# Filler matmuls against a falling TensorE clock, and a late load of the last output weights, in a decode attention kernel

## The chip, the cores and the metric

The kernel runs on one core of a Trainium2 chip. The time is the device time of one execution in microseconds (us). A profiled execution gives a trace whose span is 1.7 to 2.1 us shorter than that time; all readings at a point of time below count from the start of that span. Ratios are computed as the mean time of one kernel's fast runs over the mean of the other's fast runs in the same rounds on the same chip, so they are not quite the ratio of the medians that are quoted.

Engine names: PE is TensorE (PEld its weight loads), DVE is VectorE, ACT is ScalarE, POOL is GpSimd, SP is SyncE, which issues most of the loads.

## The reference, cut to what matters

Two attention blocks for decoding one token, batch 4, 32 query heads, 8 key/value heads of 128. Block A attends to all 8192 cached keys, block B to the last 2048. Each ends with an output projection `wo` to 512 columns.

```python
q = (x @ wq) ...                                    # 32 heads of 128
scores = einsum("bhqd,bhkd->bhqk", q, k) * Dh**-0.5 # k: (4, 8, 8192, 128), repeated 4 times over the heads
p = softmax(scores);  o = einsum("bhqk,bhkd->bhqd", p, v)
return o.reshape(B, 1, 32 * 128) @ wo               # wo: (4096, 512)
# ... block B the same with k[:, :, -2048:], v[:, :, -2048:];  the two outputs side by side
```

The caches are read once; with the weights the DMA engines move 185 MB. There is almost no arithmetic for each byte.

## The kernel before

The work is cut into 40 *units*. Units 0 to 7 are block B, units 8 to 39 are block A, one for each pair of batch row and key/value head: 2 MB of K and 2 MB of V. Unit 39 is called `L`. In each unit PE transposes K in eight jobs `T` of 1024 keys, as float32 pairs, into one of three PSUM banks; DVE and ACT by turns copy the result to SBUF; then come the scores `S` (with the query columns as the moving operand, 8 columns wide). Softmax follows on DVE, POOL and ACT, and the V products `PV` (4 columns wide) of a unit run inside the next unit.

```python
TOKENS = [("T", 0), ("T", 1), ("OT",), ("T", 2), ("T", 3), ("S", 0), ("S", 1), ("X",),
          ("T", 4), ("T", 5), ("S", 2), ("S", 3), ("PV", 0), ("PV", 1), ("OL",),
          ("T", 6), ("T", 7), ("S", 4), ("S", 5), ("PV", 2), ("PV", 3), ("S", 6), ("S", 7), ("OPJ",)]

def pe_T(u, k):
    # ... bank, slot
    def fn(pe):
        ins = None
        for pi in range(4):
            t0 = k * 8 + 2 * pi
            ins = pe.transpose(out=bkf[:, pi * 128:(pi + 1) * 128],
                               in_=K_sbf[:, slot, t0:t0 + 2, :].rearrange("p t d -> p (t d)"), identity=identf[:, :])
        return ins
    op("pe", fn, waits=[("K", u) if k == 0 else None, bankfree(idx), ("setup",)], inc=("T", idx))
```

Every fourth unit (13, 17, ..., 37) also transposes the attention output of a finished group of four units (`OT`, `OL`) and multiplies it by that group's output weights (`OPJ`, four matmuls of 512 columns). It is called a *group unit* here. Unit 37, the third last, is one. Units 10 to 37 are one loop on PE, four units a turn.

After the last unit PE finishes without further transposes. Each of the last unit's four V chunks has a semaphore of its own:

```python
for c in range(NQ): pe_PV(L - 1, c)
add(dve_norm(L - 1))
for c in range(NQ): pe_PV(L, c)
add(dve_norm(L))
pe_OPJ(L // Bn)                       # the direct form: two halves of 256 columns, four heads each
# ... add of each half to the other groups' sum, and two output DMAs

for hf in range(2):                   # the direct form in pe_OPJ
    # four matmuls, one for each head, into the bank of half hf
    op("pe", fn2, waits=[...norms of the four units..., ("W1", 3), ...], inc=("OPJ", gi, hf))
```

The last group's output weights (512 KB) are loaded from ACT's queue in unit 8, far ahead. K and V pass through SP's queue in order: ..., K of 37, V of 36, K of 38, K of 39, V of 37, V of 38, V of 39 in four chunks. A K slot (one of the four buffers for a unit's K) is free when the transposes of four units earlier are done.

```python
wo_at = {7: [1, 2], 8: [NG - 1]}      # NG - 1 is the last group
```

Of the kernel before, what the change touches and what calls it, by code (L numbers as in the profile page):

```python
# [14 lines left out]
def bass_concat_heads__gqa_block_cached__sliding_block_cached__decode_kernel(  # L15
# [15 lines left out]
    Bn, _, D = A_x.shape  # L31
    _, HKV, SK, DH = A_k_cache.shape
# [61 lines left out]
    with ExitStack() as es:  # L94
# [8 lines left out]
        def sm(name):  # L103
            return es.enter_context(nc.semaphore(name))
# [40 lines left out]
        sem_k = [sm("s_k%d" % i) for i in range(NKS)]  # L145
        sem_v = [sm("s_v%d" % i) for i in range(NVS)]
        sem_vl = [sm("s_vl%d" % i) for i in range(NQ)]
        sem_x = [sm("s_x0"), sm("s_x1")]
        sem_w1 = [sm("s_w1_%d" % i) for i in range(NQP)]
        s_w2 = sm("s_w2")  # L150
# [16 lines left out]
        def bank_f(i):  # L167
            return banks_f[i]
# [16 lines left out]
        def sem_of(key):  # L185
            t = key[0]
            if t in ("K", "Kh"):
                return sem_k[key[1] % NKS]
            if t in ("V", "Vh"):
                return sem_v[key[1] % NVS]  # L190
            if t == "VL":
                return sem_vl[key[1]]
            if t == "x":
                return sem_x[key[1]]
            if t == "out":
                return sem_out[key[1]]
            if t == "W1":
                return sem_w1[key[1]]
            if t == "wo":
                return sem_w1[2]  # L200
            if t == "pm":
                return s_pm if key[2] == 0 else s_pm2
            if t == "E":
                if jobs[key[1]]["kind"] in ("xT", "QP", "perm"):
                    return s_Eq
                return s_Ed if evac_eng[key[1]] == "dve" else s_Ea
            return {
                "W2": s_w2, "T": s_T, "S": s_S, "PV": s_PV, "OPJ": s_OPJ,
                "max": s_max, "sub": s_sub, "sum": s_sum, "rcp": s_rcp, "otr": s_otr,
                "ocp": s_ocp, "exp": s_exp, "ar1": s_ar1, "ar2": s_ar2, "setup": s_setup, "pset": s_setup,  # L210
                "mk": s_mk, "acp": s_acp, "mk0": s_mk0, "perm": s_perm, "rq": s_rq, "OPJc": s_opc,
            }[t]

        DMA_KEYS = ("K", "Kh", "V", "Vh", "VL", "x", "out", "W1", "W2", "wo", "mk")

        plan = {e: [] for e in ("sp", "pe", "act", "dve", "pool")}

# [2 lines left out]
        def op(eng, fn, waits=(), inc=None):  # L220
            plan[eng].append(dict(fn=fn, waits=[w for w in waits if w is not None], inc=inc, turn=turn[0]))

        def add(d):
            op(d["eng"], d["fn"], waits=d["waits"], inc=d["inc"])
# [63 lines left out]
        def pe_job_perm(P):  # L288
# [26 lines left out]
                return ins  # L315
            return dict(eng="dve", fn=efn, waits=[("T", idx)], inc=("E", idx))

        def pe_T(u, k):
            eng = "dve" if k % 2 == 0 else "act"
            idx = new_job("T", eng, u=u, k=k)  # L320
            tjob_idx[(u, k)] = idx
            tj = u * NB + k
            bk = bank_bf(KTB[jobs[idx]["bank"]])
            slot = u % NKS

            bkf = bank_f(KTB[jobs[idx]["bank"]])

            def fn(pe):
                ins = None
                for pi in range(4):  # L330
                    t0 = k * 8 + 2 * pi
                    ins = pe.transpose(out=bkf[:, pi * 128:(pi + 1) * 128],  # L332
                                       in_=K_sbf[:, slot, t0:t0 + 2, :].rearrange("p t d -> p (t d)"),
                                       identity=identf[:, :])
                return ins
            op("pe", fn, waits=[("K", u) if k == 0 else None, bankfree(idx), ("setup",)], inc=("T", idx))

            def efn(e):
                if eng == "dve":
                    return e.tensor_copy(out=KT_sb.bitcast(I32)[:, tj % NKT, :], in_=bkf.bitcast(I32)[:, :])  # L340
                return e.activation(out=KT_sb[:, tj % NKT, :], in_=bk[:, :], func=ACTF.Copy)  # L341
            return dict(eng=eng, fn=efn, waits=[("T", idx)], inc=("E", idx))
# [114 lines left out]
        def pe_OPJ(gi):  # L457
            u0 = gi * Bn
            un = units[u0]
            P, nhq, hq0 = un["P"], un["nhq"], un["hq0"]  # L460
            opb = bank_f(OPB)
            wo_view, wg = wo_of(gi)
            first = (gi == first_group[P])
            last = (gi == last_group[P]) or gi == NG - 2
            direct = u0 + Bn - 1 == L

            if direct:
                H2 = D // 2
                for hf in range(2):
                    def fn2(pe, hf=hf):  # L470
                        ins = None
                        dst = opb[0:Bn, 0:H2] if hf == 0 else bank_f(STB[0])[0:Bn, 0:H2]
                        for i in range(nhq):
                            ins = pe.matmul(out=dst, lhsT=OTg[:, i, :], rhs=wo_view[:, wg, i, hf * H2:(hf + 1) * H2],  # L474
                                            start=(i == 0), stop=(i == nhq - 1))
                        return ins
                    op("pe", fn2, waits=[norm_key[u0 + b] for b in range(Bn)] + [("W1", 3), ("acp",), ("sub", L - 1), ("sub", L)], inc=("OPJ", gi, hf))
                return

            def fn(pe):  # L480
                ins = None
                for i in range(nhq):
                    ins = pe.matmul(out=opb[0:Bn, 0:D], lhsT=OL[:, i // REP, i % REP, :], rhs=wo_view[:, wg + i // REP, i % REP, :],  # L483
                                    start=(P == 1 and first and i == 0), stop=(P == 1 and last and i == nhq - 1))
                return ins
            waits = [("E", ol_idx[gi]), ("W2", gi) if P == 1 else ("wo", gi)]
            op("pe", fn, waits=waits, inc=("OPJ", gi))
# [97 lines left out]
        def dve_norm(u):  # L585
            un = units[u]
            b, nhq, NC = un["b"], un["nhq"], un["S"] * un["CPT"]
            gi = u // Bn
            otb = bank_f(OTB[un["ot_use"] % 2])

            def fn(dve):
                return dve.tensor_tensor(out=OTg[:, 0:nhq, b], in0=otb[:, 0:NC], in1=rl_view(u),  # L592
                                         op=AluOpType.mult)
            norm_key[u] = ("otr", u)
            ot_uses[un["ot_use"]] = ("otr", u)
            return dict(eng="dve", fn=fn, waits=[("PV", u * NQ + NQ - 1), ("rcp", u)], inc=("otr", u))
# [65 lines left out]
        def wo_load(eng, gi):  # L662
            un = units[gi * Bn]
            P, ng, r0 = un["P"], un["nhq"] // REP, un["hq0"] * DH
            view, wg = wo_of(gi)
            src = WO[P][r0:r0 + ng * REP * DH, :]
            src = src.rearrange("(h p) n -> p h n", p=128) if gi == NG - 1 else src.rearrange("(g p r) n -> p g r n", p=128, r=REP)
            dst = view[:, wg, :, :] if gi == NG - 1 else view[:, wg:wg + ng, :, :]
            waits = []
            if gi > 0:  # L670
                waits.append(("T", qp_idx[(0, NQP - 1)]))
            if NG_B < gi < NG - 1:
                waits.append(("OPJ", gi - 1))
            key = ("W2", gi) if P == 1 else (("W1", 3) if gi == NG - 1 else ("wo", gi))
            return dict(eng=eng, fn=dma(dst, src), waits=waits, inc=key)

        wo_at = {7: [1, 2], 8: [NG - 1]}
        for gi in range(NG_B + 1, NG - 1):
            wo_at[4 * gi + 2] = [gi]

# [123 lines left out]
        add(dve_norm(L - 1))  # L804
        for c in range(NQ):
            pe_PV(L, c)
        add(dve_norm(L))
        pe_OPJ(L // Bn)
        H2 = D // 2
# [28 lines left out]
        for u in range(1, NU + 1):  # L838
            if u < L:
                sp_K(u)  # L840
                if u == L - 1:
                    sp_K(L)
            if u != L:
                sp_V(u - 1)
            else:
                sp_V(L - 1)
            if u == 1:
                add(wo_load("sp", 0))
            if u == 2:
                op("sp", dma(W1wq, WQ[0].rearrange("(p c) n -> p c n", p=128)),  # L850
                   waits=[("T", qp_idx[(1, NQP - 1)])], inc=("W1", 1))
            if u == outb_after:
                op("sp", dma(out[:, 0, D:2 * D], osb[0:Bn, 1, :]), waits=[("ocp", 1)], inc=("out", 1))
        op("sp", dma(out[:, 0, 0:H2], osb[0:Bn, 0, 0:H2]), waits=[("ocp", 0)], inc=("out", 0))
        op("sp", dma(out[:, 0, H2:D], osb[0:Bn, 0, H2:D]), waits=[("ocp", 2)], inc=("out", 2))

# [134 lines left out]
```

## Time and profile before

| | before |
|---|---|
| time, median | 449.64 us (448.83 to 449.87, 3 runs) |
| span of the profiled run | 447.8 us |
| DMA busy | 90% or more in slices 2 to 39 of 40 |
| PE busy, mean clock 150 to 410 us | 237 of 260 us, 0.79 |

The page's slices (40 equal parts of the span, 11.2 us each; digits are tenths, PEclk is the clock that TensorE was granted, GB/s what the DMA engines moved):

```profile
PE   0685199899676999988998998899889998988997
PEclk9996569989886899866596689867875986788596
DMA  8999999999999999999999999999999999999991
GB/s 337 411 415 438 413 421 415 420 421 423 423 422 421 425 422 425 424 429 427 427 427 430 430 424 426 430 428 427 429 426 427 426 430 429 426 424 430 430 403 65
```

The load stream is full from the second slice to the 39th. PE follows it with a clock that falls again and again. The windows view of the same kernel gives, for each stretch, its length, busy time and number of instructions of PE, PEld, DVE, ACT, POOL, the granted clock, the DMA share and GB/s:

```profile
core 0: us, PE busy (x) PEld busy (x) DVE busy (x) ACT busy (x) POOL busy (x), PEclk, DMA share, GB/s
150.00:410.00 260.00, 237.20 (x4351) 220.96 (x4350) 116.75 (x270) 117.02 (x133) 24.96 (x80) 0.79 1.01 427
410.00:424.00 14.00, 12.37 (x184) 10.47 (x180) 6.05 (x16) 4.40 (x5) 1.31 (x4) 0.60 1.00 426
```

The chain of waits (the work that ended last, followed back; start, length, what) has its last DMA here; after it there is nothing but PE and what PE waits for on other engines:

```profile
380.50 30.60 DMA K_sb<-in_A_k_cache_dram
...
411.14 1.11 PE ps L332 x8
```

PE's timeline from there (start, length, line, operation, operands, number; in brackets the idle time before it and what ended it). L332 are the transposes, L397 the V products, L474 the output matmuls:

```profile
411.14 1.09 PE L332 MATMUL ps<-identf,K_sb 128*128 128x128 f32 x8 [0.79 <-DMA K_sb<-in_A_k_cache_dram]
413.35 1.97 PE L332 MATMUL ps<-identf,K_sb 128*128 128x128 f32 x8 [0.41 <-ACT KT_sb L341]
...
424.83 2.69 PE L332 MATMUL ps<-identf,K_sb 128*128 128x128 f32 x16
...
431.81 2.08 PE L332 MATMUL ps<-identf,K_sb 128*128 128x128 f32 x16
...
438.96 0.39 PE L397 MATMUL ps<-PT,V_sb 128*128 128x4 bf16 x10
440.17 3.31 PE L397 MATMUL ps<-PT,V_sb 128*128 128x4 bf16 x118 [0.82 <-issue]
443.79 1.86 PE L474 MATMUL ps<-W,OTg 128*4 128x256 bf16 x8 [0.31 <-DVE OTg L592]
```

Read it so: the K tile of group unit 37 is there at 411.14. The unit lasts until 424.83, 13.7 us, because its transposes run at the half clock (1.97 us for eight, against 1.07 to 1.09 at the full one). Units 38 and 39 start at 424.83 and 431.81 and take 7 us each. The two last runs of V products begin at 438.96, the output matmuls at 443.79.

How late is that against the data? The fine DMA slices from 436 to 448 us (0.3 us each) show the engines running dry one after the other, the last at about 440:

```profile
DMA  7776675443333100010000000000000000000000
```

So at 443.8 PE is several microseconds behind the data. The tail, from 411 to the end, is bound by PE, in unit 37 and in the last products at a low clock.

### The profile page before, as it was taken

How to read it: one execution, taken by the hardware profiler on the slowest of the kernel's cores; microseconds unless marked ns; L12 is line 12 of the kernel's file. 1: busy time of each engine (PE TensorE's matmuls, PEld its weight loads, DVE VectorE, ACT ScalarE, POOL GpSimd, SP SyncE). 2: the span in 40 equal slices, each digit the busy share in tenths (PEclk: the TensorE clock that was granted, in tenths of full speed). 3: DMA queues.
4: the chain of work that ended last, by engine and by line, in shares of the span. 5: the costliest groups of instructions: out<-in, count | busy, mean ns of one | idle time of the engine just before them, and what ended most of it. 6: DMA issues, size and time to landing. Idle time of an engine off the chain costs nothing.

```text
span 447.8 us, 14767 instructions
## 1 busy us (share of the span) xinstructions
PE 373.4 (83%) x6783; PEld 339.4 (76%) x6783; DVE 195.9 (44%) x451; ACT 179.2 (40%) x202; POOL 40.1 (9%) x126
## 2 busy tenths in 40 slices
PE   0685199899676999988998998899889998988997
PEld 0685199768561898878898887879878987878896
DVE  0354055656440455434363444344443544344363
ACT  1163045435330464434264434334442543435261
POOL 1100000001100011000010001000110100010010
PEclk9996569989886899866596689867875986788596
DMA  8999999999999999999999999999999999999991
GB/s 337 411 415 438 413 421 415 420 421 423 423 422 421 425 422 425 424 429 427 427 427 430 430 424 426 430 428 427 429 426 427 426 430 429 426 424 430 430 403 65
DMA packets 17270, 185.01 MB, mean 413 GB/s; under 512 B 1860, under 2 KB 2392, under 8 KB 4824
## 3 DMA queue, kind: packets, MB, share of 16 engines
q1 hardware_dynamic: 15096, 178.27, 94.4%
q10 hardware_dynamic: 2080, 6.30, 3.5%
q8 instruction: 22, 0.36, 0.3%
q14 instruction: 8, 0.07, 0.0%
q0 software_dynamic: 64, 0.01, 0.0%
HBM read 184.56 MB, written 0.01 MB: 412 GB/s over the span
## 4 chain that ended last, share of the span: by engine, by line
DMA 54%; PE 35%; issue 4%; ACT 3%; DVE 2%; POOL 0%; ACTq 0%; POOLq 0%
DMA K_sb<-in_A_k_cache_dram 41%; PE ps L332 19%; DMA W<-in_A_wq_dram 7%; DMA W<-in_B_wo_dram 6%; PE ps L397 6%; PE ps L371 5%; PE ps L483 3%; ACT KT_sb L341 3%; PE ps L278 1%; DVE KT_sb L340 1%; DVE Dt L543 0%; DVE M L505 0%; ACT PT L554 0%; PE ps L474 0%; PE ps L438 0%
## 5 line engine op out<-in xcount | busy, mean ns | idle before, releaser
L341 ACT ACTIVATE KT_sb<-ps 128x1024 bf16<-128x1024 bf16 x160 | 163.0, 1023 | 244.9 <-PE ps L332 243.1
L332 PE MATMUL ps<-identf,K_sb 128*128 128x128 f32 x1280 | 217.1, 329 | 32.9 <-DMA K_sb<-in_A_k_cache_dram 17.5
L332 PEld LDWEIGHTS ps<-identf,K_sb 128*128 128x128 f32 x1280 | 179.0, 170 | 46.2 <-DMA K_sb<-in_A_k_cache_dram 18.6
L340 DVE COPY KT_sb<-ps 128x512 int32<-128x512 int32 x160 | 110.4, 690 | 138.9 <-PE ps L332 137.7
L397 PE MATMUL ps<-PT,V_sb 128*128 128x4 bf16 (+1 forms) x2560 | 76.2, 165 | 3.6 <-DMA V_sb<-in_A_v_cache_dram 1.8
L371 PEld LDWEIGHTS ps<-RQc,KT_sb 128*128 128x128 bf16 x2048 | 72.9, 100 | 4.5 <-ACT KT_sb L341 1.2
L371 PE MATMUL ps<-RQc,KT_sb 128*128 128x8 bf16 x2048 | 74.3, 167 | 0.9 <-ACT KT_sb L341 0.8
L397 PEld LDWEIGHTS ps<-PT,V_sb 128*128 128x128 bf16 x2560 | 70.8, 97 | 3.9 <-DMA V_sb<-in_A_v_cache_dram 2.0
L575 POOL PARTITION_ALL_REDUCE LB<-L x40 | 17.3, 432 | 155.2 <-DVE L L566 155.2
L514 POOL PARTITION_ALL_REDUCE MB<-M x32 | 11.9, 371 | 173.3 <-DVE M L505 173.3
L483 PE MATMUL ps<-W,OL 128*4 128x512 bf16 x60 | 22.5, 537 | 4.8 <-DMA W<-in_B_wo_dram 4.8
L592 DVE TENSOR_TENSOR OTg<-ps,RL 128x4 bf16<-128x4 f32 (+1 forms) x40 | 6.9, 173 | 40.2 <-PE ps L397 40.2
L505 DVE TENSOR_REDUCE M<-ps 128x4 f32<-128x256 f32 (+1 forms) x40 | 19.1, 477 | 10.8 <-PE ps L371 10.8
L566 DVE TENSOR_REDUCE L<-PT 128x4 f32<-128x256 bf16 (+1 forms) x40 | 21.9, 547 | 3.3 <-ACT PT L554 2.8
L371 PE MATMUL ps<-RQB,KT_sb 128*128 128x16 bf16 x512 | 18.6, 171 | 2.1 <-issue 1.2
L371 PEld LDWEIGHTS ps<-RQB,KT_sb 128*128 128x128 bf16 x512 | 17.9, 99 | 3.0 <-issue 1.5
L554 ACT ACTIVATE PT<-Dt 128x256 bf16<-128x256 f32 (+1 forms) x40 | 18.1, 452 | 4.0 <-DVE Dt L543 2.0
L483 PEld LDWEIGHTS ps<-W,OL 128*4 128x4 bf16 x60 | 5.6, 104 | 15.3 <-issue 8.7
L278 PE MATMUL ps<-xT,W 128*128 128x4 bf16 x256 | 7.4, 165 | 10.9 <-DMA W<-in_A_wq_dram 10.6
L278 PEld LDWEIGHTS ps<-xT,W 128*128 128x128 bf16 x256 | 7.0, 101 | 11.1 <-DMA W<-in_A_wq_dram 10.7
L543 DVE TENSOR_TENSOR Dt<-ps,MB 128x256 f32<-128x256 f32 x32 | 13.3, 415 | 0.5 <-POOL MB L514 0.5
L257 PE MATMUL ps<-ident,xo_sb 4*128 4x4 bf16 x8 | 0.6, 170 | 14.2 <-POOL identf L617 14.2
(49 smaller groups left out, 64.6 us busy)
## 6 DMA issues: line engine op xcount, KB each, us to landing
K_sb<-in_A_k_cache_dram SPq DMA_DIRECT2D x32, 2048.0 KB, 32.0
V_sb<-in_A_v_cache_dram SPq DMA_DIRECT2D x31, 2048.0 KB, 36.0
K_sb<-in_B_k_cache_dram SPq DMA_DIRECT2D x16, 1024.0 KB, 28.2
V_sb<-in_B_v_cache_dram SPq DMA_DIRECT2D x16, 1024.0 KB, 28.2
W<-in_B_wq_dram SPq DMA_DIRECT2D x1, 4096.0 KB, 12.9
W<-in_A_wq_dram SPq DMA_DIRECT2D x1, 4096.0 KB, 30.0
W<-in_A_wo_dram ACTq DMA_DIRECT2D x8, 512.0 KB, 10.5
W<-in_B_wo_dram SPq DMA_DIRECT2D x1, 2048.0 KB, 29.1
```

Of the source, the lines that this page charges most:

```text
L278: ins = pe.matmul(out=bk[:, hl * Bn:(hl + 1) * Bn], lhsT=W1wq[:, c, hq * DH:(hq + 1) * DH], rhs=xT[:, P, c, :], start=(c == 0), stop=(c == ...
L332: ins = pe.transpose(out=bkf[:, pi * 128:(pi + 1) * 128], in_=K_sbf[:, slot, t0:t0 + 2, :].rearrange("p t d -> p (t d)"), identity=identf[ ...
L340: return e.tensor_copy(out=KT_sb.bitcast(I32)[:, tj % NKT, :], in_=bkf.bitcast(I32)[:, :])
L341: return e.activation(out=KT_sb[:, tj % NKT, :], in_=bk[:, :], func=ACTF.Copy)
L371: ins = pe.matmul(out=stb[:, t * CPT:(t + 2) * CPT], lhsT=ktv[:, pi, :, e], rhs=rhs, start=(e == 0), stop=(e == 1))
L397: ins = pe.matmul(out=otb[:, s * CPT:(s + 1) * CPT], lhsT=V_sb[:, vs, t, :], rhs=pt_cols(u, t * CPT, CPT), start=(j == 0), stop=(j == J - 1))
L483: ins = pe.matmul(out=opb[0:Bn, 0:D], lhsT=OL[:, i // REP, i % REP, :], rhs=wo_view[:, wg + i // REP, i % REP, :], start=(P == 1 and first ...
L505: return dve.tensor_reduce(out=M1[:, 0:NC].rearrange("p (s h) -> p s h", h=CPT), in_=stb[:, 0:NT * CPT].rearrange("p (s j h) -> p s h j", ...
L543: return dve.tensor_tensor(out=Dt[:, 0:NT * CPT].rearrange("p (s j h) -> p s j h", s=S, h=CPT), in0=stb[:, 0:NT * CPT].rearrange("p (s j h ...
L554: return act.activation(out=PT[:, u % NPT, 0:NW], in_=Dt[:, 0:NW], func=ACTF.Exp, scale=scale)
L566: return dve.tensor_reduce(out=L1[:, 0:NC].rearrange("p (s h) -> p s h", h=CPT), in_=PT[:, u % NPT, 0:NT * CPT].rearrange("p (s j h) -> p ...
L575: return pool.partition_all_reduce(LB[:, 0:NC], L1[:, 0:NC], channels=128, reduce_op=ReduceOp.add)
```

## The change

Two intents. First, TensorE's clock falls when its activity is thin; a wide dummy matmul ("filler", 128x512 into the bank that the next transposes overwrite) ahead of every second transpose job, and two fillers after each of the last unit's first three V chunks, should keep it up. Second, the last output weights are not needed until the very end: as the last transfers, one head each with its own semaphore, they let all K and V data land earlier. The output matmuls then go head by head.

```diff
+        def filler(pe, bk):
+            return pe.matmul(out=bk[:, 0:512], lhsT=ident[:, :], rhs=RQA[:, :, :, :, :].rearrange("p b g e c -> p (b g e c)"),
+                             start=True, stop=True)
+        def pe_filler(n): ...          # n fillers into the bank of the last job, after its evacuation
@@ pe_T
             def fn(pe):
                 ins = None
+                if u >= LB0 and k % 2 == 0:          # LB0 is 10
+                    filler(pe, bkf)
                 for pi in range(4):
@@ pe_OPJ, direct
-                for hf in range(2):
-                    ...four heads...   waits=[..., ("W1", 3), ...], inc=("OPJ", gi, hf))
+                for i in range(nhq):
+                    for hf in range(2):
+                        ...one matmul... waits=[..., ("WL", i), ...], inc=("OPJ", gi, hf) if i == nhq - 1 else None)
@@
-        wo_at = {7: [1, 2], 8: [NG - 1]}
+        wo_at = {7: [1, 2]}
@@ the end of PE's program
             pe_PV(L, c)
+            if c < NQ - 1:
+                pe_filler(2)
@@ the end of SP's queue, after V of the last unit
+        for i in range(REP):
+            op("sp", dma(wl_view[:, wl_g, i, :], wl_src[:, i, :]), waits=[("T", qp_idx[(0, NQP - 1)])], inc=("WL", i))
```

## The prediction

> **What bounds the kernel now.** The page's slices show the DMA engines at 90% or more up to slice 39, at 420 to 430 GB/s. K tiles land about 30 us after issue (issue list): some six 2 MB loads are always queued; a unit's K and V (4 MB) take 9.8 us. PE follows: in the windows view a warm unit takes 7 us (424.5 to 431.8), a cold one 10 or more; the granted clock over 200 to 400 us is 0.70 to 0.82.
>
> The time is the stream plus the tail. From the third-last K (411.14, last DMA in the chain of waits) PE runs without waiting for data: its group unit stays cold for 13 us (411 to 424.5: clock 0.56, eight transposes 1.97 us against 1.07 warm). The last two K tiles land (issue plus latency) at 420.9 and 425.8; PE reaches them at 424.8 and 431.8. Unit L's scores end at 439.1, when nearly all data are there (fine DMA slices: engines drain unevenly from 433, the last at 440.1). Then, cold again, V products run to 443.5, eight output matmuls (1.86 us) to 445.65; 2.1 us more to the end. The tail is late through PE, not data.
>
> **What the change does.**
> - 120 fillers (units 10 to 39, four each), one 128x512 bf16 matmul each. The existing projections of that size cost 0.25 us warm (four in 1.02) and 0.45 cold (four in 1.86): 1.0 to 1.8 us a unit. A warm unit becomes 8 us, under 9.8; a cold one about 12, over the stream.
> - Do they wake the clock? [...] The Trainium skill ("TensorE: Matmul & The Clock Gate", Part 4) says that transposes do not count as busy the same way[...]. I expect a mean of about 0.9, with dips at waits for K.
> - Two fillers after each of the first three V chunks: 0.5 us, in gaps of 1.2 us between landings; output matmuls stay warm (0.8 us).
> - 512 KB of output weights move from the eighth unit to the end of SP's queue. The stream ends as before, but K and V land 1.2 us earlier (0.52 MB at 427 GB/s), and the weights under the last V products.
> - Both output halves finish together, so their adds queue: plus 0.4 us.
>
> **Sum.** Last V chunk at about 438.9 instead of 440.1, PE ready before it; V products and norm to 439.8; last weights at 440.1 to 440.6; last output matmul about 442 against 445.65; plus 0.4. Gain 3 to 4 us if the clock holds, 1 to 2 if not throughout. Predicted 446.3 us, range 444.3 to 449.0. Chances: faster by over 2% 0.02, within 2% 0.94, slower 0.04.
>
> **What the profile would show.** Right: DMA full to slice 39; mean clock near 0.9, no cold unit after 411; PE waiting for the last K and V chunks; output matmuls released by the weights' DMA, last before 443. Wrong: eight transposes still 1.97 us; SP waiting longer and DMA below 420 GB/s.
>
> **What would make it wrong.** Fillers that do not wake the clock make PE the bound (460 us or more). Weights landing slowly would eat the gain. Over 2% would need a shorter stream, which nothing here gives.

## The result, and the profile after

| | before | after |
|---|---|---|
| time, median | 449.69 us (4 runs) | 454.17 us (452.50 to 454.69, 4 runs) |
| ratio of the fast runs | | 1.0094, 95% interval 1.0074 to 1.0114 |
| span of the profiled run | 447.8 us | 452.9 us |
| mean clock, 150 to 410 us | 0.79 | 0.87 |

The kernel became 0.9% slower, where a gain of 3 us was predicted. That is less than the 2% at which the runs are classed as different, but clear of the noise. (The median of before is that of the table above with one run more; the profiled run after is the slowest of its four.) The page's slices after (11.3 us each):

```profile
PEclk9996569887975899998898789689969876895595
DMA  8999999999999999999999999999999999999970
```

The stream is as full as before and ends as early (the 39th slice, which ends at 441.6 us, is the last with data). In the windows view the clock is higher in the body of the kernel, at the same 427 GB/s, and lower where it matters:

```profile
150.00:410.00 260.00, 242.32 (x4482) 219.40 (x4481) 120.18 (x273) 118.84 (x135) 25.45 (x81) 0.87 1.01 427
410.00:424.00 14.00, 13.07 (x170) 11.27 (x171) 5.22 (x14) 4.40 (x5) 0.57 (x2) 0.50 1.01 428
```

In shorter windows, not copied here, the clock falls at 409.01, just as PE runs out of work and begins to wait for K, and stays at 0.50 until 429.49. The chain of waits again has its last DMA at the third-last K, and then PE:

```profile
380.58 29.45 DMA K_sb<-in_A_k_cache_dram
...
410.08 0.61 PE ps L322
```

PE's timeline after (L322 are the fillers, L351 the transposes, L416 the V products, L492 the output matmuls):

```profile
410.08 0.61 PE L322 MATMUL ps<-RQA,ident 128*128 128x512 bf16 x1 [1.07 <-DMA K_sb<-in_A_k_cache_dram]
410.48 1.91 PE L351 MATMUL ps<-identf,K_sb 128*128 128x128 f32 x8
...
426.04 0.61 PE L322 MATMUL ps<-RQA,ident 128*128 128x512 bf16 x1
...
434.38 0.38 PE L322 MATMUL ps<-RQA,ident 128*128 128x512 bf16 x1
...
441.95 1.78 PE L416 MATMUL ps<-PT,V_sb 128*128 128x4 bf16 x64
444.02 0.57 PE L416 MATMUL ps<-PT,V_sb 128*128 128x4 bf16 x16 [0.29 <-issue]
444.45 1.01 PE L322 MATMUL ps<-RQA,ident 128*128 128x512 bf16 x2
445.26 0.61 PE L416 MATMUL ps<-PT,V_sb 128*128 128x4 bf16 x16
...
448.74 1.87 PE L492 MATMUL ps<-W,OTg 128*4 128x256 bf16 x8 [0.31 <-DVE OTg L610]
```

The first fillers run at 0.4 us apart from the transposes behind them (410.08 to 410.48), so each costs PE 0.4 us at the low clock; at the full clock it is 0.2 us (starts of a filler and of its transposes). The difference of the two spans, 5.1 us, splits exactly along these points of the two timelines:

| stretch of the tail | before | after | difference |
|---|---|---|---|
| third-last K reached at | 411.14 | 410.08 | -1.06 |
| group unit 37, until unit 38 starts | 13.69 | 15.96 | +2.27 |
| unit 38, until unit 39 starts | 6.98 | 8.34 | +1.36 |
| unit 39, until the V products of 38 | 7.15 | 7.57 | +0.42 |
| V products of 38 and 39, until the first output matmul | 4.83 | 6.79 | +1.96 |
| output matmuls to the end | 4.01 | 4.16 | +0.15 |

The data do arrive about 1.1 us earlier. Everything after that is PE, and PE now has 18 fillers in its way.

### The profile page after: what moved, and what is told of

Its sections match the earlier page's. It is cut to its first block, busy times and chain, and to the rows that moved or that the text cites. A ratio compares the mean times of both kernels' runs of the same rounds, so it can differ in the third digit from the quotient of the medians.

```text
span 452.9 us, 15022 instructions
## 1 busy us (share of the span) xinstructions
PE 383.4 (85%) x6909; PEld 339.5 (75%) x6909; DVE 197.0 (44%) x451; ACT 179.8 (40%) x202; POOL 40.3 (9%) x126
## 4 chain that ended last, share of the span: by engine, by line
DMA 46%; PE 45%; issue 4%; ACT 3%; DVE 2%; POOL 0%; DVEq 0%; POOLq 0%; ACTq 0%
DMA K_sb<-in_A_k_cache_dram 33%; PE ps L351 21%; PE ps L416 7%; DMA W<-in_A_wq_dram 7%; DMA W<-in_B_wo_dram 6%; PE ps L390 6%; PE ps L322 5%; PE ps L501 3%; ACT KT_sb L360 2%; PE ps L281 1%; DVE KT_sb L359 0%; PE ps L492 0%; PE ps L457 0%; DVE Dt L561 0%; DVE M L523 0%
## 5 line engine op out<-in xcount | busy, mean ns | idle before, releaser
L351 PE MATMUL ps<-identf,K_sb 128*128 128x128 f32 x1280 | 202.3, 311 | 7.4 <-DMA K_sb<-in_B_k_cache_dram 4.3
L351 PEld LDWEIGHTS ps<-identf,K_sb 128*128 128x128 f32 x1280 | 178.2, 163 | 24.4 <-issue 6.9
L416 PE MATMUL ps<-PT,V_sb 128*128 128x4 bf16 (+1 forms) x2560 | 76.5, 165 | 3.2 <-DMA V_sb<-in_A_v_cache_dram 2.9
L416 PEld LDWEIGHTS ps<-PT,V_sb 128*128 128x128 bf16 x2560 | 71.3, 97 | 5.3 <-DMA V_sb<-in_A_v_cache_dram 3.3
L390 PE MATMUL ps<-RQc,KT_sb 128*128 128x8 bf16 x2048 | 70.8, 167 | 0.8 <-ACT KT_sb L360 0.8
L390 PEld LDWEIGHTS ps<-RQc,KT_sb 128*128 128x128 bf16 x2048 | 69.4, 98 | 2.6 <-ACT KT_sb L360 0.9
L322 PE MATMUL ps<-RQA,ident 128*128 128x512 bf16 x126 | 56.1, 450 | 17.9 <-issue 7.5
L322 PEld LDWEIGHTS ps<-RQA,ident 128*128 128x128 bf16 x126 | 12.6, 102 | 24.1 <-issue 11.8
L501 PE MATMUL ps<-W,OL 128*4 128x512 bf16 x60 | 21.0, 508 | 8.7 <-DMA W<-in_B_wo_dram 8.7
L281 PE MATMUL ps<-xT,W 128*128 128x4 bf16 x256 | 7.4, 165 | 10.9 <-DMA W<-in_A_wq_dram 10.6
```

What stands on the lines that cost most here:

```text
L281: ins = pe.matmul(out=bk[:, hl * Bn:(hl + 1) * Bn], lhsT=W1wq[:, c, hq * DH:(hq + 1) * DH], rhs=xT[:, P, c, :], start=(c == 0), stop=(c == ...
L322: return pe.matmul(out=bk[:, 0:512], lhsT=ident[:, :], rhs=RQA[:, :, :, :, :].rearrange("p b g e c -> p (b g e c)"), start=True, stop=True)
L351: ins = pe.transpose(out=bkf[:, pi * 128:(pi + 1) * 128], in_=K_sbf[:, slot, t0:t0 + 2, :].rearrange("p t d -> p (t d)"), identity=identf[ ...
L390: ins = pe.matmul(out=stb[:, t * CPT:(t + 2) * CPT], lhsT=ktv[:, pi, :, e], rhs=rhs, start=(e == 0), stop=(e == 1))
L416: ins = pe.matmul(out=otb[:, s * CPT:(s + 1) * CPT], lhsT=V_sb[:, vs, t, :], rhs=pt_cols(u, t * CPT, CPT), start=(j == 0), stop=(j == J - 1))
L501: ins = pe.matmul(out=opb[0:Bn, 0:D], lhsT=OL[:, i // REP, i % REP, :], rhs=wo_view[:, wg + i // REP, i % REP, :], start=(P == 1 and first ...
```

## The experiments

Theory A: the tail is a chain of PE work that starts when the third-last K lands. Fillers there are plain cost, since they do not raise the clock where it falls; the moved weights bring their 1.1 us. Theory B: the moved weights hurt, as the output matmuls wait for them or the last loads slow down. Theory C: the fillers in the body delay the release of K buffers and so slow the stream. And the intended effect: fillers hold the clock.

Each kernel was timed in five rounds beside the kernel before, and all results were correct. These are the times and, from PE's timeline of each profiled run, the starts of the same points of the tail. They are single traces; the times are the evidence, the traces say where to look.

| run | time, median | ratio to before, 95% | K of 37 reached | unit 38 | unit 39 | V products of 38 | output matmuls | span |
|---|---|---|---|---|---|---|---|---|
| before | 449.64 | | 411.14 | 424.83 | 431.81 | 438.96 | 443.79 | 447.8 |
| after | 454.17 | 1.0094 (1.0074 to 1.0114) | 410.08 | 426.04 | 434.38 | 441.95 | 448.74 | 452.9 |
| e1_weights_alone | 448.37 | 0.9973 (0.9953 to 0.9993) | 409.87 | 423.80 | 431.45 | 438.60 | 443.11 | 447.2 |
| e2_tfill_alone | 452.57 | 1.0069 (1.0052 to 1.0086) | 411.28 | 427.24 | 435.66 | 443.23 | 447.46 | 451.4 |
| e3_vfill_alone | 452.38 | 1.0071 (1.0056 to 1.0086) | 411.87 | 425.92 | 433.56 | 440.71 | 447.43 | 450.6 |
| e4_after_no_vfill | 451.71 | 1.0042 (1.0022 to 1.0062) | 410.20 | 424.15 | 432.48 | 440.62 | 444.87 | 449.0 |
| e5_body_only | 448.95 | 0.9993 (0.9973 to 1.0013) | 410.25 | 422.64 | 430.28 | 438.05 | 442.21 | 446.3 |
| e6_last2_only | 448.92 | 0.9986 (0.9959 to 1.0012) | 409.92 | 424.00 | 430.76 | 438.33 | 443.03 | 447.2 |
| e7_half_by_half | 448.06 | 0.9966 (0.9945 to 0.9988) | 410.13 | 423.93 | 430.49 | 437.65 | 442.33 | 446.3 |
| e8_bursts | 446.88 | 0.9942 (0.9923 to 0.9961) | 410.23 | 421.16 | 427.83 | 434.98 | 441.07 | 445.2 |
| e9_group_beside4 | 449.15 | 1.0001 (0.9971 to 1.0031) | 410.32 | 424.71 | 432.36 | 439.51 | 444.16 | 448.3 |
| e10_group_beside8 | 449.28 | 0.9998 (0.9973 to 1.0024) | 410.77 | 423.90 | 431.44 | 438.59 | 443.46 | 447.6 |
| e11_bursts_and_v | 449.54 | 1.0018 (0.9994 to 1.0042) | 410.17 | 420.95 | 427.20 | 434.67 | 441.81 | 445.9 |
| e12_burst_before_k | 446.50 | 0.9942 (0.9921 to 0.9964) | 410.39 | 421.14 | 428.62 | 435.77 | 440.75 | 444.9 |

e1 to e4 shared one set of runs of before (median 449.55), e5 to e8 another (449.53), e9 to e12 a third (449.21). "K of 37 reached" is the first transpose or filler behind the wait for K that has a record. In e9 and e10, and for "unit 38" in e6, a filler ahead of it has no record, so these points are about 0.4 us late.

### First four: the change taken apart

**e1_weights_alone**: the changed kernel without any filler.

```diff
-                if u >= LB0 and k % 2 == 0:
-                    filler(pe, bkf)
-            if c < NQ - 1:
-                pe_filler(2)
```

> The move of the last output weights alone (four head loads at the end, output matmuls head by head), no fillers. Theory A (the tail is PE work after the landing of the third-last K, and the change only brings data about 1.1 us earlier): the third-last K lands near 410.1 instead of 411.1 in the profile, the end comes 0.5 to 1.0 us earlier (the two adds now run one after the other, +0.35), time about 449.0, ratio 0.998. Theory B (weights at the very end delay the output matmuls or slow the last loads): same time or 1 to 3 us slower, with the output matmuls released by the weights' DMA.

Measured: 448.37 us, 0.27% faster than before. The third-last K is reached at 409.87, and the output matmuls follow the norm after 0.30 us, as before: no wait for the weights. Theory B falls. The step of the prediction about the weights (data 1.2 us earlier, bytes unchanged) holds.

**e2_tfill_alone**: the kernel before, with the transpose fillers only.

```diff
+                if u >= LB0 and k % 2 == 0:
+                    filler(pe, bkf)
```

> Only the filler ahead of every second transpose job, nothing else. Theory A (fillers cost in the tail only, where PE is the bound and the clock stays cold): the third-last K lands near 411 as before, the group unit after it stays cold and takes about 2 us more, the two last units about 2 us more: time 452 to 453.5, ratio 1.006. Theory C (fillers slow the stream, through later releases of K buffers): the third-last K lands later than 412. Intended effect (they wake the clock): time 446 to 448.

Measured: 452.57 us, 0.69% slower: 3 us for a thing that was meant to speed up. The third-last K is reached at 411.28 against 411.14, so the stream is not delayed by what the profile shows (150 to 410 us: 427 GB/s in both). The group unit takes 15.96 us, the same as in the changed kernel, and 13.69 before.

**e3_vfill_alone**: the kernel before, with the six fillers between V chunks only.

```diff
+            if c < NQ - 1:
+                pe_filler(2)
```

> Only the two fillers after each of the first three V chunks of the last unit. Theory A: V chunks have landed, six fillers run cold at about 0.43 us on the chain: last output matmul 2.6 us later, ratio 1.006, and the output matmuls no faster than 1.86 us for eight. Intended effect: they fall into gaps between landings and the output matmuls take about 1 us for eight: the same time or 0.8 us faster.

Measured: 452.38 us, 0.71% slower. Their timeline shows both what they cost and what they give (L411 V products, L319 fillers, L488 output matmuls):

```profile
443.19 1.02 PE L319 MATMUL ps<-RQA,ident 128*128 128x512 bf16 x2
444.00 0.61 PE L411 MATMUL ps<-PT,V_sb 128*128 128x4 bf16 x16
444.47 1.01 PE L319 MATMUL ps<-RQA,ident 128*128 128x512 bf16 x2
...
447.43 1.03 PE L488 MATMUL ps<-W,OTg 128*4 128x256 bf16 x8 [0.31 <-DVE OTg L606]
```

From one V chunk to the next it takes 1.28 us (443.19 to 444.47), of which 0.41 us are V products; the chunks are in SBUF long before. Three such pairs are 2.6 us. In return the clock is up for the eight output matmuls here, 1.03 us in place of 1.86, so the expectation that they would stay at 1.86 missed in this trace; in the changed kernel itself they did stay at 1.87. One trace doesn't give the whole 2.8 us: from the V products of 38 to the end it is 1.05 us longer than before (450.6 - 440.71 against 447.8 - 438.96), and the rest stands ahead of any filler, where this run was later than the one of before (its clock stayed low until 429.51, that of before until 426.37). The times of six runs, and the two other pairs with and without these fillers (after against e4, e11 against e8: 2.5 and 2.7 us), put the cost at 2.5 to 2.8 us.

**e4_after_no_vfill**: the changed kernel without the six fillers.

```diff
-            if c < NQ - 1:
-                pe_filler(2)
```

> The changed kernel without the six fillers between V chunks. Theory A: 2.6 us less than the changed kernel, about 451.5, ratio to before 1.004; what is left is the transpose fillers of the last three units (+2.5) less the earlier data (-0.8). Theory B/C: stays at 453 to 454.

Measured: 451.71 us. The times of e4 lie some 1 us further above their spans than those of the other runs, so its trace understates its time. The parts add up within the intervals: -0.27% (weights), +0.69% (transpose fillers) and +0.71% (V fillers) make +1.13%, measured +0.94%. In this run's trace the clock came back inside the group unit (the last transposes there took 1.04 us for eight), so the fillers do sometimes wake it; not reliably, as the times of e4 lie between 450.05 and 452.38. From the V products of unit 38 to the first output matmul it takes 4.25 us, against 6.79 in the changed kernel: as much as the 2.5 us between the two medians (the spans of the two profiled runs differ by 3.9 us, about 1 us of it for the reason just given).

### Second four: where the transpose fillers cost, and whether any filler can pay

**e5_body_only**: moved weights, and the transpose fillers only in three of the four units of a turn of the loop, so none in units 37, 38 and 39.

```diff
-                if u >= LB0 and k % 2 == 0:
+                if LB0 <= u < LB1 and (u - LB0) % NLB != NLB - 1 and k % 2 == 0:
```

> Moved weights, and transpose fillers in three of four units of the loop (84 of 120), but none in the last three units and none between V chunks. Theory A (fillers cost only in the tail): same as the moved weights alone, ratio 0.997, although the mean clock from 150 to 410 us is higher than 0.79. Theory C (they slow the stream): ratio 1.000 or more and the third-last K later than 411.

Measured: 448.95 us, ratio 0.9993 against 0.9973 for the weights alone. The intervals overlap, so this run leaves open whether the 84 fillers of the body cost nothing or up to about 1 us. The mean clock from 150 to 410 us is 0.86 in place of 0.79, and the stream runs at 427 GB/s all the same: a higher clock there buys nothing, and the first point of theory A, that the body's clock is not the bound, stands. Theory C in its strong form (the stream slows) falls: the third-last K is reached at 410.25, without a wait in this trace, because PE came from a cold unit. The clock fell in group unit 37 all the same, at 412.60, so a wait for K is not needed for that.

**e6_last2_only**: moved weights, and the fillers in units 38 and 39 only.

```diff
-                if u >= LB0 and k % 2 == 0:
+                if u >= LB1 and k % 2 == 0:          # LB1 is 38
```

> Moved weights, and transpose fillers in the last two units only (8). Theory A: units 38 and 39 take about 1.9 us longer on PE (1.5 while the clock wakes, 0.4 when it is up), ratio about 1.0015 against 0.9973 for the weights alone. Theory C: no more than 0.3 us over the weights alone.

Measured: 448.92 us, 0.0013 in the ratio above the weights alone, about 0.6 us and within the intervals, where 1.9 us was expected: a miss in size. In its trace the clock was up from 424.64, and unit 38 took 6.8 us, or about 7.2 with the filler ahead of it that has no record; without fillers there it takes 6.3 to 7.7 us in the other traces. Unit 39 took 7.57 us at the full clock in place of 7.15: four fillers of 0.21 us cost 0.42 there, so about half of them was hidden. Behind what was not tested. A filler at the low clock takes 0.4 us.

**e7_half_by_half**: moved weights, with the output matmuls in the order of before.

```diff
-                for i in range(nhq):
-                    for hf in range(2):
-                        ...one matmul...
+                for hf in range(2):
+                    ...four heads...  waits=[..., ("WL", 0), ("WL", 1), ("WL", 2), ("WL", 3), ...], inc=("OPJ", gi, hf))
```

> Moved weights, but the output matmuls half by half as before, so that the add of the first half runs beside the matmuls of the second. Theory A: the weights have landed when the matmuls start, so no wait for them; 0.35 us faster than head by head, ratio 0.9965. If the order by heads does hide a wait for the last head's weights, it is equal or slower.

Measured: 448.06 us, 0.0007 in the ratio below e1, 0.3 us. That has the expected sign and size, but is within the intervals, so not shown.

**e8_bursts**: moved weights; no filler beside the transposes, but five ahead of the wait for K in each group unit (the transposes that follow overwrite the bank), and three after `OT`, in a score bank that is free then.

```diff
+            burst = LB0 <= u < LB1 and (u - LB0) % NLB == NLB - 1
+            if burst and k == 0:
+                op("pe", ...five fillers into bkf..., waits=[bankfree(idx)])                     # no wait for K
+            if burst and k == 2:
+                op("pe", ...three fillers into STB[u % 2]..., waits=[("E", tjob_idx[(u, 0)])])
             op("pe", fn, waits=[("K", u) if k == 0 else None, bankfree(idx), ("setup",)], inc=("T", idx))
```

> Moved weights, and fillers only where PE idles in a group unit: five ahead of the wait for its K tile and three after the transpose of the attention output, in each group unit; none elsewhere. If the clock falls because activity is thin just before and in those gaps, the group unit after the third-last K stays warm and takes about 9 to 10 us instead of 13.7, the last V chunk then ends the tail, and the time is 445 to 446.5, ratio about 0.992. If fillers cannot hold the clock here at all, the group unit takes 14 to 16 us and the ratio is 1.000 to 1.003.

Measured: 446.88 us, ratio 0.9942. The group unit takes 10.9 us (410.23 to 421.16) in place of 13.7. From here on the V data end the tail: the last V chunk lands at 439.4, and the V products of it run 0.05 us later. Five runs lie within 0.24 us, the least scatter of all.

### Last four: number or place

**e9_group_beside4**: moved weights, and the changed kernel's four fillers, beside the transposes, in group units only.

```diff
+                if LB0 <= u < LB1 and (u - LB0) % NLB == NLB - 1 and k % 2 == 0:
+                    filler(pe, bkf)
```

> Moved weights, and the four transpose fillers in the group units only (28 in all), none in the last two units and none between V chunks. If the rest of the cost of the transpose fillers lies in the group unit after the third-last K (4 fillers of 0.4 us cold): 1.6 us over the weights alone, ratio 1.000 to 1.001. If it lies in the rest of the body, ratio 0.997.

Measured: 449.15 us, ratio 1.0001: 0.0028 or about 1.3 us above the weights alone, as expected. (e5, e6 and e9 share out the 120 transpose fillers; their costs in the ratio, 0.0020, 0.0013 and 0.0028, make 0.0061, against 0.0069 in e2.) The interval is wide (0.9971 to 1.0031) because the six runs fall in two lots, three at 448.0 to 448.3 and three at 450.0 to 451.0. In the trace, which is of one of the three longer runs, the clock fell at 407.98, 0.6 us before PE began to wait for K, and came back within the unit, at 418.22.

**e10_group_beside8**: as e9 with two fillers each time, so that a group unit has eight, as many as with the bursts.

```diff
+                    filler(pe, bkf)
+                    filler(pe, bkf)
```

> Moved weights, and eight fillers in each group unit, as many as the bursts had, but two by two ahead of the transposes of an even job, behind the wait for K. If the place decides (PE idle gaps), the clock still falls at the wait for K, the group unit takes 15 us or more and the ratio is 1.001 to 1.004. If the number decides, it is as fast as the bursts, 0.994.

Measured: 449.28 us, ratio 0.9998. The expectation was half right. The time is not that of the bursts, so the number alone does not do it. But the group unit did not take 15 us or more: 13.1 us, or about 13.5 with the first filler, for in this trace the clock fell at the wait for K (first eight transposes 1.92 us) and was up again from 413.79 (the next eight 1.04 us). In this trace the denser fillers woke it sooner, and the time was no better.

**e11_bursts_and_v**: the bursts of e8 and the six fillers between V chunks.

> The bursts of the group units with the six fillers between the last V chunks. With the bursts PE waits for the last V chunks, so the six fillers now lie in gaps: they cost nothing, the eight output matmuls take 1.05 us in place of 1.87, time 446.0, ratio 0.992. If they cost PE time as in the changed kernel: 1.5 to 2.5 us more than the bursts alone.

Measured: 449.54 us, 2.7 us more than e8, with a scatter of 3 us (447.98 to 450.96; the profiled run is the fastest of the six). The expectation that the six fillers now lie in gaps fell. PE had been idle or in narrow V products for some time, so the clock was down when they began (L322 fillers, L429 V products, L505 output matmuls):

```profile
438.80 1.01 PE L322 MATMUL ps<-RQA,ident 128*128 128x512 bf16 x2
439.61 0.61 PE L429 MATMUL ps<-PT,V_sb 128*128 128x4 bf16 x16
440.08 1.01 PE L322 MATMUL ps<-RQA,ident 128*128 128x512 bf16 x2
...
441.81 1.87 PE L505 MATMUL ps<-W,OTg 128*4 128x256 bf16 x8 [0.31 <-DVE OTg L623]
```

A chunk with its two fillers takes 1.28 us at that clock, as long as a chunk needs to land (524,288 bytes at 427 GB/s are 1.2 us). There is no gap to lie in, and the output matmuls stay at 1.87 us.

**e12_burst_before_k**: e8 without the three fillers after `OT`; only the five ahead of the wait for K.

```diff
-            if burst and k == 2:
-                op("pe", ...three fillers into STB[u % 2]...)
```

> Moved weights, and only the five fillers ahead of the wait for K in group units, without the three after the attention output's transpose. If the gap at K alone makes the clock fall, it is as fast as both bursts (0.994). If the second gap (waiting for ACT) also does, the clock falls near 412 and the ratio is 0.996 to 0.998.

Measured: 446.50 us, ratio 0.9942, the same as e8: 2.7 us faster than before in the same rounds, and about 7.7 us faster than the changed kernel, which ran in others. So the three fillers after `OT` are not needed; those ahead of the wait for K are enough. That the gap as such makes the clock fall is not shown by this, and the count below speaks against it. The timeline and the chain of waits (L349 transposes, L429 V products, L505 output matmuls; one of the five fillers has no record, as some matmul records are missing in a trace):

```profile
409.07 1.02 PE L322 MATMUL ps<-RQA,ident 128*128 128x512 bf16 x4
410.39 1.09 PE L349 MATMUL ps<-identf,K_sb 128*128 128x128 f32 x8 [0.30 <-DMA K_sb<-in_A_k_cache_dram]
...
412.60 1.09 PE L349 MATMUL ps<-identf,K_sb 128*128 128x128 f32 x8 [0.46 <-ACT KT_sb L373]
```

```profile
409.94 29.87 DMA V_sb<-in_A_v_cache_dram
439.81 0.05 issue
439.86 0.60 PE ps L429 x16
...
440.75 1.66 PE ps L505 x7
```

The fillers end at 410.09, PE then still waits 0.30 us for K, and eight transposes take 1.09 us through the whole unit, where before they took 1.97. They cost nothing, for they lie in time in which PE had to wait anyway. The clock does fall later, at 421.38, and unit 38 begins cold, but the V data end the tail all the same. And the last link but PE's few products is now the last V chunk: the tail is bound by data, which is what the whole change was after.

### Where the clock changes: a count over the traces

This was counted after the runs, from the clock and the busy times in the windows view; no run was made to test it. Outside the short windows in which it changes, the clock is either 1.00 or 0.50. Between 150 and 446 us it changes 429 times in the 14 traces, and in each trace all changes lie, to 0.02 us, on one grid of 3.41 us. Where the grid lies differs from trace to trace. So the clock can be read stretch by stretch. For the 76 whole stretches from 180.6 to 440.0 us in the trace of before, sum the busy time of the transposes and the 512-column matmuls and leave out the matmuls of 4 and 8 columns:

| clock in the stretch | clock after it | stretches | summed busy time |
|---|---|---|---|
| full | full | 25 | 1.46 us or more |
| full | half | 15 | 1.40 us or less |
| half | half | 21 | 2.60 us or less |
| half | full | 15 | 2.96 us or more |

The lots do not overlap. With borders at 1.43 and 2.78 us, fitted to the traces, 24 of the 1159 stretches of all 14 traces fall on the wrong side, among them some in which fillers have no record. Idle time as such does not decide: 54 of the 209 falls came after a stretch in which PE was busy for 3.40 us or more, among them the fall before unit 37 in the changed kernel (405.60 to 409.01: PE busy 3.41 us, the sum 1.41) and in e9 (404.56 to 407.98: 3.42 and 1.38). In unit 37 of the changed kernel the five cold stretches sum to 2.46 to 2.53 us, four of them from eight transposes (1.91) and one filler (0.6): too little to bring the clock back. In e12 the stretch with the burst (407.72 to 411.14) sums to 1.77, of which the transposes are 0.75, and the clock stays up.

## Why the prediction was wrong

- **The bound was read rightly.** Full stream, and a tail late through PE from the third-last K on: e1 to e12 all agree with it.
- **The weights were right.** Predicted 1.2 us earlier data; 1.06 in the changed kernel, and 0.27% (1.2 us) in e1. The 0.4 us for the two adds in a row is in the table as part of +0.15 (the other part is that the matmuls are not faster); e7 has the sign, not the proof.
- **The first step that failed: "no cold unit after 411".** The prediction asked whether the fillers wake the clock, and answered with two readings: that cold stretches of 10 us ended at a group unit's four 512-column matmuls, and that sixteen transposes in a row ended at the full clock. In the trace those two stretches lasted 17.1 and 13.7 us, the clock rose about 2 us after the four matmuls (224.98 and 426.37), and the sixteen transposes ran at half clock throughout (3.68 us from 401.37; the clock rose at 405.89). From this it let 120 fillers lift the mean clock to about 0.9 and took that for the tail too. The mean clock did rise, 0.79 to 0.87 from 150 to 410 us, where it is worth nothing. In group unit 37 it was 0.50, lower than before. Predicted for this unit and the two after it: about the full clock, with PE ready before the last data. Measured: +2.27, +1.36 and +0.42 us. What showed the danger was in the trace before: cold stretches there began near PE's wait for K, and the fillers stood behind that wait. In the changed kernel the clock had already fallen when the first filler of unit 37 started, and one filler to eight transposes was too little to bring it back. The profile showed the prediction's own sign for "wrong": eight transposes at 1.91 us. e12 puts the fillers ahead of the wait, and the clock holds. With 410 to 424 us at 0.91 in its windows view, and 0.50 in that of the changed kernel, the place is shown to matter; e10 shows that the number is not enough.
- **The second step that failed: "in gaps of 1.2 us between landings".** The prediction placed the last V chunks against PE as it would be if the first step held. As it did not, the chunks had landed, and six fillers at about 0.43 us were on the chain: +0.71% alone (e3). e11 shows that it would have failed even with the first step right: at the low clock two fillers and a chunk's products take 1.28 us. The 0.8 us hoped for from warm output matmuls was seen in e3 only, and by luck: there all three pairs of fillers fell into one stretch of the grid, and the clock rose at its end (446.58).
- **The cost of a filler was sized rightly** (predicted 0.45 us cold and 0.25 warm, measured 0.4 and 0.2), but it was set against the stream alone ("a warm unit becomes 8 us, under 9.8"). In the tail there is no stream to hide behind. The prediction had said that the tail is PE's, and then costed the fillers as if PE had slack there.
- **What stays open.** Whether the body's fillers cost up to about 1 us (e5). What the clock really counts: the sums above fit the traces, but no run set out to test them. And 0.78 us in e8 ahead of its output matmuls, which its profile gives to "issue"; in e12 it is 0.09 us.

The prediction's own number, 446.3 us, came out in e12 (446.5 us). That is another kernel: its tail ends with the last V chunk, as was predicted, but through fillers in another place and with output matmuls still cold (1.86 us).

## What to carry to other kernels

A dummy matmul is only free in time in which the engine has to wait anyway, so put it ahead of the wait and not behind it, and ask of each stretch, not of the whole kernel, whether there is such time. In these traces the clock followed the time in transposes and 512-column matmuls in each 3.41 us, not how busy PE was, so count those. A higher mean clock is no gain where the stream is the bound; look at the clock in the stretch where the engine is the bound, which is often the tail. And where one part of a change is meant to make room for another (the V fillers' gaps), work out what the second costs if the first does not happen.

## What the Trainium skill lacked or had wrong

- "TensorE: Matmul & The Clock Gate", Why this matters for your kernels: it asks for no idle gaps over about 3 us between bursts of matmuls. That is not enough here. In the changed kernel the clock fell at 409.01, at the start of an idle gap of 1.07 us and after 1.6 us of matmuls of 4 and 8 columns; in e9 it fell at 407.98 with PE busy all through the 3.41 us before. Five 512-column matmuls ahead of the wait (e12) held it. The page does not say how narrow matmuls count; here they did not seem to count at all.
- The same page, Part 1, What's actually happening: about 3.4 us of sustained activity release the clock. In the changed kernel PE was busy for 12.65 of the 13.5 us from 411 to 424.5 by its windows view, and the clock stayed at 0.50 until 429.49. The busy share of a profile is not the activity that counts, and the page gives no measure of it. In the trace of before, 2.96 us or more of transposes and 512-column matmuls in a stretch of 3.41 us brought the clock back, and 2.60 us or less did not.
- The same page, Part 4, PE-mode transpose: the full clock does not engage for transposes, as they do not count as busy in the same way. For the transposes of this kernel (float32, 128x128) the traces say otherwise: in the kernel before, the stretch from 320.55 to 323.97 held sixteen of them and almost nothing else, and the clock rose at its end; in e12 a unit of 32 transposes and narrow matmuls kept the full clock for about 9 us once it was up.
- "DMA: Bandwidth & Descriptors", Queues, rings and completion order: each engine takes a ring's descriptors in order. The runs are in line with it: with 0.5 MB taken from ACT's queue in unit 8 and put behind K and V in SP's, the third-last K was there 1.06 us earlier in the changed kernel. The page gives no figure for how far apart the 16 engines finish a stream; here they ran dry over about 6 us, from 434 to 440.
